# Attention with a memory term, then routed experts, on one core: K and Q turned by TensorE instead of the DMA queue, and one pool of five PSUM banks

## The chip, the cores and the metric

The kernel runs on one core of a Trainium2 chip. The metric is the device time of one execution in microseconds (us). A core has TensorE (PE in the rows; PEld is its weight load), VectorE (DVE), ScalarE (ACT), GpSimd (POOL) and SyncE (SP), which here only issues DMAs, one after the other in the order in which they stand in its program. Sixteen DMA engines move the data.

## The reference

Inputs are q, k and v of shape 8 x 8 x 576 x 64 (batches, heads, rows, depth), a memory M of 64 x 64 and a vector z per batch and head, and the weights of eight experts. In brief:

```python
scores = q @ k.T / 8                       # causal, 576 x 576 per head
local  = softmax(scores) @ v
q_p    = where(q > 0, q, exp(q) - 1) + 1   # phi
mem    = (q_p @ M) / (q_p @ z)
x      = g * mem + (1 - g) * local         # g = sigmoid(beta), per head
# routing: the 4608 rows of x go to 8 experts of capacity 576, best score first
out[rows of e] = maximum(x @ w1[e], 0) @ w2[e]
```

The order of the routing depends on x @ w_gate, so the attention has to be precise: each float32 number is carried as two float16 halves, high and low (`h` and `l` in the names).

## The kernel before, in words

The program has two parts. `attention` works through 16 units; a unit is four heads of one batch. `moe_all` follows it and is not touched by the change.

In a unit K, Q and V are loaded (`kf`, `qf`, `vf`, 32-bit). ACT, DVE or POOL split them: the high half is a cast, the low half a subtraction. The two halves of K stand side by side in a tile `h16` of 18 blocks of 128 columns, and likewise those of Q; both have to be turned (rows to columns) before TensorE can use them. The turned tiles are `kT` and `qT`. In units 1 to 15 one DMA transpose of all 18 blocks does it (line 794); in unit 0 TensorE does it (line 787) and the blocks are copied out of PSUM. Then 64 partitions of `kT` are copied into `kB` (DVE) and 64 partitions of `qT` into `qM` (ACT). phi of Q goes the same way into `pT`, by a DMA transpose.

Then come the maxima: TensorE multiplies `qM` by `kT` into a PSUM bank (`pm`), DVE reduces the bank (line 807), 13 banks in a unit. The maxima are turned and written into row 64 of `qM` by a small DMA (line 866), so that the scores come out with the maximum subtracted. The scores go into PSUM banks `st`, twelve in a unit; ACT takes exp of each twice, once to float16 (`ph`, line 941) and once to float32 (lines 945, 948), and the difference `pl` is made by DVE (line 946) or POOL (line 949). `ph` and `pl` times V, and phi times M, gather in `avs`; DVE divides (lines 988 to 999), the result is split again into `xs`, turned by a DMA transpose into `xT` (line 1008) for the gate logits, and written to DRAM as `xd`.

PSUM has two banks `pm` (maxima, small turnings, logits), three banks `st` (scores, turnings of unit 0) and three for `avs`.

The order of everything in `attention` comes from a planner, `Sched`. Each piece of work is a node with the engines that it may run on and a cost in ns on each; `run` places one node after the other by earliest start and by priority. The priorities are tables of numbers (`PR['off']`, and `PR['dl']` for single units); `PR['bias']` and `PR['pin']` choose between engines. Only the order and the choice of engine reach the chip: each engine then executes its own list in that order and waits by semaphores.

Of the kernel before, what the change touches and what calls it, by code (L numbers as in the profile page):

```python
# [8 lines left out]
F32 = mybir.dt.float32  # L9
# [14 lines left out]
          'kba': -12673.13,  # L24
          'kbd': 29586.98,
          'kbv': -25704.42,
          'kha': -15364.72,
          'khp': -12539.24,
          'khv': -3684.87,
          'klp': -5840.71,  # L30
          'klv': -5300.46,
          'mh2a': -3643.2,
          'mh2v': -10560.2,
          'mha': 4609.58,
          'mhv': 3127.63,
          'mlp': 10679.73,
          'mlv': 10869.94,
          'mra': -14972.51,
          'mrv': -26064.0,
          'mza': 11663.77,  # L40
          'mzv': 5122.68,
          'nap': -923.34,
          'nav': -3267.9,
          'nca': -3175.08,
          'ncp': 457.98,
          'ncv': -3705.71,
          'nsp': -4400.74,
          'nsv': 7885.89,
          'p2p': 3448.83,
          'p2v': -5.41,  # L50
          'p4sp': -16452.05,
          'p4sv': -7016.64,
          'pha': 888.22,
          'php': 8134.1,
          'phra': -13218.83,
          'phrv': 14272.35,
          'phv': -6326.42,
          'plp': 4097.89,
          'plv': 4394.03,
          'prepca': -4983.65,  # L60
          'prepcv': 10793.59,
          'qha': -15522.63,
          'qhp': -3121.95,
          'qhv': 2344.84,
          'qlp': -238.04,
          'qlv': 12285.04,
          'qmovea': 2067.13,
          'qmovev': -1201.49,
          'tea': -3562.47,
          'tev': -3884.84,  # L70
          'vha': 10327.79,
          'vhp': -9961.82,
          'vhv': -5992.86,
          'vlp': -5727.56,
          'vlv': 6154.88,
          'xtea': -11851.0,
          'xtev': -7724.13},
 'dl': {'0': {'AV': 85.12,
              'MX': -176.12,
              'N': -174.88,  # L80
              'P2': -232.53,
              'S': -115.14,
              'fin1': 7.89,
              'fin2': 136.19,
              'kb': -101.7,
              'kh': -240.29,
              'kl': -254.81,
              'kt': -109.58,
              'lk': -219.52,
              'lm': -178.54,  # L90
              'lq': -173.13,
              'lv': -176.91,
              'maxrem': -181.54,
              'mfin': 1.0,
              'mfin2': -278.46,
              'mfin3': -235.61,
              'mh': -252.27,
              'ml': 217.86,
              'mz': -301.17,
              'nadd': -276.57,  # L100
              'ncast': -70.14,
              'nsub': -175.89,
              'ph': -94.62,
              'phe': -545.98,
              'phr': -91.1,
              'phs': -192.45,
              'pl': -160.08,
# [1381 lines left out]
```

## Time and profile before

| | us |
|---|---|
| median of three runs | 992.35 (989.7 to 994.24) |
| the profiled execution, its own time | 989.19 |
| its span, first to last instruction | 987.4 |
| attention, 0 to 517 us of the span | 517 |
| experts, from 517 us on | 470.4 |

Over the span PE is busy 80%, DVE 73%, ACT 59% and POOL 54%; the mean granted TensorE clock is 0.914 of full speed. These shares mix the two parts, so the attention is read on its own below.

### The profile page before, as it was taken

What the parts mean: (1) busy time and instruction counts of PE and PEld (TensorE: products, weight loads), DVE (VectorE), ACT (ScalarE), POOL (GpSimd) and SP (SyncE); (2) the same over time, 40 slices, a digit from 0 to 9 for tenths busy, and PEclk for the clock granted to TensorE, in tenths of its full rate; (3) what the DMA queues carried; (4) which work ended last, traced back from release to release, by engine and by line L of the source; (5) the groups of instructions that cost most, each with busy time, mean ns of one, the idle gap of its engine ahead of it and who ended that gap; (6) DMA issues with size and microseconds to landing.
All of it is one profiled execution on the core that took longest, in us unless ns stands there. A gap on an engine that the chain in (4) does not pass through costs nothing.

```text
span 987.4 us, 23446 instructions
## 1 busy us (share of the span) xinstructions
PE 788.5 (80%) x8908; PEld 494.3 (50%) x8908; DVE 724.1 (73%) x2355; ACT 585.4 (59%) x1010; POOL 537.2 (54%) x492
## 2 busy tenths in 40 slices
PE   3466777867777787677861389999999999999995
PEld 2254555656656566555650254444444444444442
DVE  8888889978889898788878887787787777702010
ACT  4366766658777787656743376574746574655110
POOL 6357766757678775645630134655554555496101
PEclk9986979879899899979995599999999999999998
DMA  5679777989888888875240506363647354693101
GB/s 131 98 150 180 156 153 151 191 160 168 171 154 174 158 167 173 164 146 119 39 105 11 213 7 221 101 220 100 216 106 230 86 204 118 224 269 106 46 12 37
DMA packets 336583, 139.08 MB, mean 141 GB/s; under 512 B 306262, under 2 KB 315478, under 8 KB 336470
## 3 DMA queue, kind: packets, MB, share of 16 engines
q1 hardware_dynamic: 330581, 118.71, 53.2%
q0 software_dynamic: 5888, 18.88, 5.8%
q8 instruction: 69, 1.13, 0.5%
q14 instruction: 45, 0.36, 0.1%
HBM read 72.40 MB, written 18.87 MB: 92 GB/s over the span
## 4 chain that ended last, share of the span: by engine, by line
PE 54%; DVE 21%; DMA 9%; issue 5%; SPq 4%; POOL 3%; ACT 3%; POOLq 0%; DVEq 0%; ACTq 0%
PE py L1138 19%; PE ph L1138 17%; PE avs L647 7%; PE st L647 4%; DVE mx L807 4%; PE pm L647 3%; DVE xt L999 2%; PE prem L1138 2%; SPq L707 2%; DMA xT<-xs 2%; DVE pl L946 2%; DVE scr L1372 2%; DMA qT<-h 2%; DMA pT<-p 1%; DMA kT<-h 1%
## 5 line engine op out<-in xcount | busy, mean ns | idle before, releaser
L1288 POOL TENSOR_TENSOR wl<-wst,wh 128x1024 f16<-128x1024 f32 x60 | 128.3, 2166 | 90.8 <-ACT wh L1287 76.6
L1138 PE MATMUL ph<-xT,wh 128*128 128x512 f16 (+1 forms) x560 | 162.7, 365 | 0.4 <-DVE hl L1331 0.4
L807 DVE TENSOR_REDUCE mx<-pm 128x1 f32<-128x512 f32 (+4 forms) x273 | 134.1, 525 | 14.5 <-PE pm L647 14.2
L941 ACT ACTIVATE ph<-st 128x512 f16<-128x512 f32 x192 | 114.1, 594 | 48.0 <-PE st L647 19.7
L647 PE MATMUL st<-qT,kT 128*128 128x64 f16 (+3 forms) x576 | 112.1, 258 | 26.9 <-DVE pl L946 20.6
L949 POOL TENSOR_TENSOR pl<-pf,ph 128x512 f16<-128x512 f32 x80 | 95.2, 1194 | 61.8 <-ACT pf L948 53.5
L647 PE MATMUL avs<-V,ph 128*128 128x65 f16 x1792 | 114.5, 203 | 17.1 <-DVE de L988 5.2
L647 PE MATMUL pm<-kT,qM 128*128 128x384 f16 (+5 forms) x384 | 91.1, 329 | 39.6 <-DVE mx L807 21.7
L647 PEld LDWEIGHTS <-ph 128*128 128x128 f16 x1792 | 104.2, 105 | 26.3 <-issue 23.0
L647 PE MATMUL avs<-V,pl 128*128 128x65 f16 x896 | 109.6, 206 | 0.0
L647 PE MATMUL st<-qM,kB 128*128 128x64 f16 (+3 forms) x576 | 107.6, 257 | 2.1 <-DMA qM<-mrx 1.8
L1350 POOL DMA_INDIRECT out_dram<-ys,idx x40 | 39.0, 976 | 109.8 <-ACT ys L1345 57.8
L1138 PE MATMUL ph<-xT,wl 128*128 128x512 f16 (+1 forms) x280 | 98.4, 365 | 0.0
L1138 PE MATMUL py<-wh,hh 128*128 128x512 f16 x256 | 97.0, 379 | 0.0
L1138 PE MATMUL py<-wl,hh 128*128 128x512 f16 x256 | 97.0, 379 | 0.0
L1138 PEld LDWEIGHTS <-wh 128*128 128x128 f16 x1072 | 68.2, 98 | 57.1 <-issue 1.9
L1138 PE MATMUL prem<-xT,wh 128*128 128x64 f16 x512 | 96.6, 193 | 0.0
L1330 ACT ACTIVATE hh<-ph 128x512 f16<-128x512 f32 x64 | 38.0, 595 | 92.3 <-PE ph L1138 69.0
L647 PEld LDWEIGHTS <-pl 128*128 128x128 f16 x896 | 91.2, 105 | 0.0
L1331 DVE SCALAR_TENSOR_TENSOR hl<-ph,hh 128x512 f16<-128x512 f32 x64 | 43.8, 686 | 60.5 <-ACT hh L1330 59.7
L1372 DVE TENSOR_SCALAR_CACHE_REDUCE scr<-p_LwT,th 128x320 f16<-128x320 f32 x168 | 85.2, 543 | 2.5
L647 PEld LDWEIGHTS <-identb 128*128 128x128 bf16 (+1 forms) x640 | 61.6, 109 | 45.5 <-issue 33.1
(283 smaller groups left out, 2122.2 us busy)
## 6 DMA issues: line engine op xcount, KB each, us to landing
wst<-in_moe_w_dram SPq DMA_DIRECT2D x32, 1024.0 KB
kf<-in_k_dram SPq DMA_DIRECT2D x64, 128.0 KB
qf<-in_q_dram SPq DMA_DIRECT2D x64, 128.0 KB
vf<-in_v_dram SPq DMA_DIRECT2D x64, 128.0 KB
xd<-xs SPq DMA_DIRECT2D x16, 512.0 KB
kf<-in_k_dram SPq DMA_DIRECT2D x32, 32.0 KB
qf<-in_q_dram SPq DMA_DIRECT2D x32, 32.0 KB
mf<-in_M_prev_dram SPq DMA_DIRECT2D x16, 64.0 KB
```

The costliest lines, as they stand in the source:

```text
L647: def MM(*a,**kw): mm(*a,skip_group_check=True,**kw)
L707: SC.add('l'+nm,dq(728,hw=450),lambda x,h=h,s=s: nc.sync.dma_start(out=t[:,4*h:4*h+4,:],in_=s),w=K(nm+'f',u%2,4*h,4*h+4),prio=pr('l'+nm,u, ...
L807: R=lambda o,i: nc.vector.tensor_reduce(o,i,axis=mybir.AxisListType.X,op=ALU.max)
L941: c=SC.add('Eh',[('A',478)],lambda x,a=a: nc.scalar.activation(phs_[x.buf['ph']][:,0:512],stb[a.buf['st']],AF.Exp,scale=0.125),acq=('ph',) ...
L946: e=SC.add('P2v',[('V',602)],lambda x,a=a,c=c: nc.vector.tensor_sub(pls_[c.buf['ph']][:,0:512],stb[a.buf['st']],phs_[c.buf['ph']][:,0:512] ...
L949: e=SC.add('P2',[('P',1113)],lambda x,c=c,d=d: nc.gpsimd.tensor_sub(pls_[c.buf['ph']][:,0:512],pfs[d.buf['pf']],phs_[c.buf['ph']][:,0:512] ...
L1138: def MM(*a,**kw): mm(*a,skip_group_check=True,**kw)
L1288: SC.add('sp',[('P',2079)],lambda x,ws=ws,k=k,s=s: G_.tensor_sub(wl[:,k,s],ws(),wh[:,k,s]),r=[key+('h',)],w=[key+('l',)],after=[b],rel=rel ...
L1330: b=SC.add('hh',[('A',478)],lambda x,a0=a0,f=f: A_.activation(hh[:,f],phb[a0.buf['ph']],AF.Relu),w=[('hh',f)],after=[y],prio=pr('hh',n,pos ...
L1331: SC.add('hl',[('V',602)],lambda x,a0=a0,f=f: V_.scalar_tensor_tensor(hl[:,f],phb[a0.buf['ph']],0.0,hh[:,f],op0=ALU.max,op1=ALU.subtract), ...
L1350: z=SC.add('scat',[('P',655 if i<4 else 330,'p',0,(1034,'n'))],lambda x,e=e,i=i,r_=r_: G_.indirect_dma_start(out=out,out_offset=bass.Indir ...
L1372: V(462,lambda x,j=j,t_=t_,c_=c_: V_.tensor_scalar(scr[j],LwT,t_[:,j+1:j+2],0.0,op0=ALU.is_ge,op1=ALU.add,accum_out=c_[:,j:j+1]),r=['LwT', ...
```

## The change

The halves of K and Q of every unit are turned by TensorE, in pieces of 8, 8 and 2 blocks, and copied from PSUM into `kT` and `qT` by ACT or DVE. `qT` to `qM` may now be moved by a DMA, and is, in units 1 to 15. phi and the outputs are still turned by the DMA queue. `pm` and `st` become one pool `pb` of five banks. Low halves are made in pieces of 8 and 10 blocks instead of 9 and 9. The planner's costs for DMAs and for two other nodes are changed, and its tables are new: `dl` has entries for all 16 units, and `pin` puts other work on other engines.

```diff
-    def run(self,tol=100,sem=170,same=110,t0=0.0,hwg=450,dlat=1300,dend=950,ph=2800.0,thr=3060):
+    def run(self,tol=100,sem=170,same=110,t0=0.0,hwg=450,dlat=1300,dend=950,ph=2800.0,thr=3060,pel=60):
...
-                    st_=max(dmaf,q); free[e]=st_+1089 if kind=='t' else s2+25
+                    st_=max(dmaf,q); free[e]=st_+1500 if kind=='t' else s2+25
...
-    pmb=[ps.tile([128,512],F32,name=f'pm{i}') for i in range(2)]; stb=[ps.tile([128,512],F32,name=f'st{i}') for i in range(3)]
+    pbb=[ps.tile([128,512],F32,name=f'pb{i}') for i in range(5)]
...
-            SC.add('l'+nm,dq(728,hw=450),lambda x,h=h,s=s: nc.sync.dma_start(out=t[:,4*h:4*h+4,:],in_=s),
+            SC.add('l'+nm,dq(728,hw=530),lambda x,h=h,s=s: nc.sync.dma_start(out=t[:,4*h:4*h+4,:],in_=s),
...
+    def PTT(u): return UO(u).get('ptt') or P_.get('ptt','')
+    def MVP(u): return PCP(u) if u==0 else P_.get('mvp') or [[0,18]]
+    def PCP(u): return UO(u).get('pc_p') or P_.get('pc_p') or [[0,8],[8,16],[16,18]]
...
-            if nm in UO(u).get('ptt',''):
+            if nm in PTT(u):
...
-                        p=stb[x.buf['st']].bitcast(F16)
+                        p=pbb[x.buf['pb']].bitcast(F16)
                         for i in range(a,b_): nc.tensor.transpose(p[:,128*(i-a):128*(i-a)+128],g()[:,i],cst['idh'])
...
-                x_=SC.add(nm+'t',dq(112*(b_-a),kind='t'),lambda x,a=a,b_=b_: nc.sync.dma_start_transpose(
+                x_=SC.add(nm+'t',dq(176*(b_-a),kind='t'),lambda x,a=a,b_=b_: nc.sync.dma_start_transpose(
...
-            SC.add('qmove',al('qmove',u,v=..,a=..), ... cp(x.var,qM[u%3][0:64,a:b_],qTs[U3][64:128,a:b_])
+            SC.add('qmove',al('qmove',u,d=819*(b_-a)/18+60,v=..,a=..), ... nc.sync.dma_start(out=qM[u%3][0:64,a:b_],in_=qTs[U3][64:128,a:b_]) if x.var=='d' else cp(...)
...
-                n3=SC.add('N3',[('V',680)],f,
+                n3=SC.add('N3',[('V',970)],f,
...
- 'pin': {'kh': 'a', 'ph': 'a', 'phr': 'a', 'vh': 'a', 'qmove': 'a', 'ns': 'p**v',
+ 'pin': {'kh': '*', 'ph': 'p', 'phr': 'v', 'vh': 'p', 'qmove': 'dvvv', 'ns': 'ppp*', 'te': '*a*aa*a**aa*',
...
+ 'ptt': 'kq',
```

Every `pmb` and `stb` of the rest becomes `pbb`.

Three places show what moves. The first is SP's list in the middle of the attention (`kf`, `qf`, `vf` are loads, `xd` the outputs; 128x18x128 is a whole unit). Before:

```order
L794 DMA_TRANSPOSE pT_122<-p_115 128x18x128
L707 DMA vf_109<-in_v_dram 128x4x64 x2
L711 DMA vf_109<-in_v_dram 64x2x64 x2
L707 DMA kf_104<-in_k_dram 128x4x64 x4
L712 DMA kf_104<-in_k_dram 64x2x64 x2
L1008 DMA_TRANSPOSE xT_167<-xs_165 128x20x128
L794 DMA_TRANSPOSE qT_121<-h_113 128x18x128
L804 DMA qM_100<-qM_100 1x16x144
L1021 DMA xd<-xs_165 64x512
L1022 DMA xd<-xs_165 128x4x512
L794 DMA_TRANSPOSE kT_118<-h_114 128x18x128
```

The same part of SP's list in the changed kernel:

```order
L1200 DMA_TRANSPOSE pT_123<-p_115 128x18x128
L1169 DMA mf_125<-in_M_prev_dram 64x4x64
L1110 DMA vf_109<-in_v_dram 128x4x64 x4
L1114 DMA vf_109<-in_v_dram 64x2x64 x2
L1414 DMA_TRANSPOSE xT_168<-xs_164 128x20x128
L1210 DMA qM_99<-qM_99 1x16x144
L1427 DMA xd<-xs_164 64x512
L1428 DMA xd<-xs_164 128x4x512
L1208 DMA qM_99<-qT_120 64x2304
L1110 DMA qf_107<-in_q_dram 128x4x64 x4
```

Two of the four transposes of a unit are gone, and a move of 64 partitions (line 1208) stands in the list instead; over the whole list 15 + 15 transposes leave and 15 moves come.

The second place is ACT's list, again in the middle. Before, the exps of the scores with the move of Q and the cast of V between them:

```order
L877 ACTIVATE ef_110<-ef_110 128x1152
L689 COPY qM_98<-qT_119 64x2304
L941 ACTIVATE ph_130<-st_175 128x512
L689 CAST V_101<-vf_108 128x20x64
L945 ACTIVATE st_175<-st_175 128x512
L941 ACTIVATE ph_136<-st_176 128x512
```

After:

```order
L1321 ACTIVATE p4h_151<-pb_176 128x128
L1347 ACTIVATE ph_131<-pb_177 128x512
L1322 ACTIVATE p4f<-pb_176 128x128
L1092 COPY kT_116<-pb_173 128x1024
L1092 COPY kT_116<-pb_174 128x256
L1347 ACTIVATE ph_134<-pb_175 128x512
```

The move of Q and the cast of V have left ACT, and the copies of the turned blocks out of PSUM have come: 60 of 128x1024 and 30 of 128x256 in the program, all on ACT, beside eight smaller ones of unit 0.

The third place is DVE's list (`mx` are the reductions of the maxima, `xt` and `de` the division, `pl` a low half of the scores). Before:

```order
L807 TENSOR_REDUCE mx_155<-pm_174 128x1
L996 TENSOR_TENSOR xt_162<-avs,de_160 128x320
L807 TENSOR_REDUCE mx_155<-pm_173 128x1
L946 TENSOR_TENSOR pl_143<-st_175,ph_135 128x512
L1033 COPY lt_170<-pm_174 128x40
L999 SCALAR_TENSOR_TENSOR xt_162<-avs,de_160,xt_162 128x64 x5
L1037 TENSOR_TENSOR lt_170<-lt_170,pm_174 128x40
L807 TENSOR_REDUCE mx_155<-pm_173 128x1 x2
```

After:

```order
L1405 SCALAR_TENSOR_TENSOR xt_162<-avs,de_160,xt_162 128x64 x5
L1213 TENSOR_REDUCE mx_156<-pb_177 128x1
L1213 TENSOR_REDUCE mx_156<-pb_174 128x1 x2
L1213 TENSOR_REDUCE mx_156<-pb_173 128x1
L1213 TENSOR_REDUCE mx_156<-pb_175 128x1 x2
L1213 TENSOR_REDUCE mx_156<-pb_176 128x2
L1213 TENSOR_REDUCE mx_156<-pb_174 128x1
```

Before, other work stands between nearly all the reductions; after, those of a unit follow one another over all five banks. In TensorE's list the 209 banks of maxima came in 82 runs of one bank, 46 of two and six longer ones before, a run being what stands between two pieces of scores or products; after there are 24 of one, 10 of two and 32 longer ones, of up to 13. The last maxima stand eight heads ahead of the end before, and twelve after.

Summed over the lists, DVE issues 2051 instructions before and 2068 after, ACT 928 and 942, POOL 497 and 541. Per unit 1 to 15 the casts of V and phi go from ACT to POOL, the relu of phi from ACT to DVE; 15 subtractions `xs` go from DVE to POOL, and low halves of K from DVE (6 to 2) to POOL.

## Rows read from the trace of the kernel before

**Rows 1.** Busy time of each engine in two stretches, the attention and the experts: stretch in us, its length, busy us (instructions) by engine, then the granted clock, the share of the DMA engines and GB/s.
```profile
0.00:517.00 517.00, 370.89 (x6077) 287.25 (x6077) 437.47 (x1109) 348.34 (x600) 330.65 (x351) 0.89 0.76 148
517.00:987.40 470.40, 417.57 (x2831) 207.09 (x2831) 286.65 (x1246) 237.11 (x411) 206.53 (x141) 0.94 0.42 133
```

**Rows 2.** The instructions in order of time, ACT: the small cast that ends the maxima of a unit, of unit 1 and of unit 15 (start, duration).
```profile
67.31 0.25 ACT L689 CAST mr<-pm 18x128 f16<-18x128 f32 x1
...
482.14 0.25 ACT L689 CAST mr<-pm 18x128 f16<-18x128 f32 x1 [1.02 <-PE pm L859]
```

**Rows 3.** Busy time between those two casts and behind the second (columns PE, PEld, DVE, ACT, POOL, clock, DMA share, GB/s), and in the stretch where DVE is busiest.
```profile
67.31:482.14 414.83, 311.18 (x5157) 243.15 (x5157) 353.58 (x898) 294.55 (x506) 279.32 (x272) 0.87 0.81 158
482.14:517.40 35.26, 24.27 (x556) 20.64 (x553) 26.70 (x88) 20.33 (x41) 15.90 (x17) 0.99 0.40 75
...
350.00:375.00 25.00, 20.66 (x400) 16.54 (x399) 23.82 (x63) 19.89 (x36) 17.96 (x17) 1.00 0.89 171
```

**Rows 4.** SP's list in order of time: start, duration of the issue, what is issued.
```profile
262.74 3.42 SPq L794 DMA_TRANSPOSE qT<-h  x1
266.25 0.61 SPq L804 DMA_DIRECT2D qM<-qM  x1
266.92 0.58 SPq L1021 DMA_DIRECT2D xd<-xs  x1
267.55 0.58 SPq L1022 DMA_DIRECT2D xd<-xs  x1
268.18 3.72 SPq L794 DMA_TRANSPOSE kT<-h  x1
271.95 1.17 SPq L707 DMA_DIRECT2D kf<-in_k_dram  x2
273.16 2.23 SPq L712 DMA_DIRECT2D kf<-in_k_dram  x2
```

**Rows 5.** The same issues by line, over the whole program: min/median/max in ns, first and last start.
```profile
L794 SPq DMA_TRANSPOSE kT<-h x15: 2704/2856/4440, 25.4 to 431.2; - x15
L794 SPq DMA_TRANSPOSE qT<-h x15: 2621/3005/3582, 38.8 to 445.7; - x15
L794 SPq DMA_TRANSPOSE pT<-p x17: 1231/3104/4651, 21.2 to 476.8; - x17
L1008 SPq DMA_TRANSPOSE xT<-xs x15: 3038/3120/3652, 87.6 to 498.9; - x15
L707 SPq DMA_DIRECT2D kf<-in_k_dram x64: 448/513/1577, 0.7 to 398.0; - x64
L712 SPq DMA_DIRECT2D kf<-in_k_dram x32: 599/607/1521, 1.8 to 399.3; - x32
```

**Rows 6.** The chain that ended last, by line, as shares of the span.
```profile
PE py L1138 19%; PE ph L1138 17%; PE avs L647 7%; PE st L647 4%; DVE mx L807 4%; PE pm L647 3%; DVE xt L999 2%; PE prem L1138 2%; SPq L707 2%; DMA xT<-xs 2%; DVE pl L946 2%; DVE scr L1372 2%; DMA qT<-h 2%; DMA pT<-p 1%; DMA kT<-h 1%
```

**Rows 7.** DMA around one transpose of 18 blocks, which is issued at 476.84 us and has nothing beside it: stretches as in rows 1.
```profile
478.00:480.00 2.00, 1.02 (x19) 0.75 (x18) 1.87 (x6) 2.00 (x5) 1.99 (x3) 1.00 1.17 196
480.00:482.00 2.00, 1.73 (x36) 1.35 (x35) 1.94 (x8) 0.67 (x2) 1.46 (x2) 1.00 0.57 99
```

**Rows 8.** ACT's groups, shapes apart: count, busy us and mean ns, idle time before them.
```profile
L689 ACT COPY qM<-qT 64x2304 f16<-64x2304 f16 x15 | 31.7, 2110 | 17.3 <-DMA qT<-h 17.1
L689 ACT CAST V<-vf 128x1280 f16<-128x1280 f32 x15 | 19.4, 1293 | 2.6 <-PE avs L647 2.5
L876 ACT ACTIVATE ef<-qf 128x1152 f32<-128x1152 f32 x15 | 17.5, 1165 | 2.7 <-POOL p L778 2.5
L689 ACT CAST p<-ef 128x1152 f16<-128x1152 f32 x15 | 17.3, 1152 | 31.1 <-DVE ef L878 18.9 <-DMA pT<-p 12.3
L689 ACT COPY xT<-pm 128x640 f16<-128x640 f16 x3 | 2.1, 692 | 2.9 <-PE pm L1017 2.9
L1258 ACT COPY xT<-py 128x512 f16<-128x512 f16 x5 | 2.8, 586 | 7.3 <-DVE xT L1257 7.3
```

**Rows 9.** Groups of DVE and POOL, likewise.
```profile
L1002 DVE TENSOR_TENSOR xs<-xt,xs 128x320 f16<-128x320 f32 x15 | 10.3, 690 | 0.1
L690 DVE CAST h<-qf 128x1152 f16<-128x1152 f32 x15 | 13.2, 878 | 5.9 <-DMA qT<-h 3.8 <-issue 1.5 <-DMA xd<-xs 0.6
L778 DVE TENSOR_TENSOR h<-kf,h 128x576 f16<-128x576 f32 x6 | 8.9, 1488 | 0.0
L691 POOL TENSOR_SCALAR V<-vf 128x768 f16<-128x768 f32 x1 | 0.8, 842 | 0.0
L691 POOL TENSOR_SCALAR V<-vf 128x512 f16<-128x512 f32 x1 | 0.6, 624 | 0.0
L1002 POOL TENSOR_TENSOR xs<-xt,xs 128x320 f16<-128x320 f32 x49 | 45.3, 927 | 38.2 <-DVE xs L690 26.0 <-ACT xs L689 8.7 <-PE avs L647 2.7
```

**Rows 10.** Turnings on TensorE that are there already: 36 blocks of unit 0 and 20 of the last outputs (groups), and five of the latter in order of time (start, length of the run of five).
```profile
L787 PE MATMUL st<-idh,h 128*128 128x128 f16 x36 | 4.7, 308 | 9.7 <-POOL h L778 8.7 <-DVE qT L690 0.9
L1017 PE MATMUL pm<-idh,xs 128*128 128x128 f16 x20 | 1.8, 218 | 2.4 <-DVE xs L690 2.3
...
507.61 0.44 PE L1017 MATMUL pm<-idh,xs 128*128 128x128 f16 x5
```

**Rows 11.** The first step of the division on DVE, in order of time: the first and the last of the eight heads behind the last maxima.
```profile
483.26 0.17 DVE L988 SCALAR_TENSOR_TENSOR de<-avs,eps 128x10 f32<-128x10 f32 x1 [0.50 <-PE avs L647]
...
512.69 0.17 DVE L988 SCALAR_TENSOR_TENSOR de<-avs,eps 128x10 f32<-128x10 f32 x1 [1.67 <-PE avs L647]
```

More of the change, by code (lines that the diff above doesn't have):

```diff
@@ L41 @@
-          'mzv': 5122.68,
+          'kba': -26568.09,
+          'kbd': 40635.67,
+          'kbv': -61697.16,
+          'kha': -51687.37,
+          'khp': 22485.47,
+          'khv': -5643.82,
+          'klp': -44101.74,
+          'klv': -46879.6,
+          'mh2a': 23202.08,
+          'mh2v': 41742.42,
+          'mha': -803.96,
+          'mhv': -17250.11,
+          'mlp': 32467.03,
+          'mlv': 3444.98,
+          'mra': 23705.05,
+          'mrv': -33461.43,
+          'mza': -15047.4,
@@ new lines @@
+          'p4sp': -13422.2,
+          'p4sv': 18348.44,
+          'pha': -2666.63,
+          'php': 109708.75,
+          'phra': 29855.7,
+          'phrv': 24082.96,
+          'phv': 1286.06,
+          'plp': 4127.93,
+          'plv': 4521.49,
+          'prepca': -28993.02,
+          'prepcv': -42440.6,
+          'qha': -15602.67,
+          'qhp': 56435.17,
+          'qhv': 61680.59,
+          'qlp': -22555.44,
+          'qlv': 26102.73,
+          'qmovea': 25183.32,
+          'qmoved': -25040.81,
@@ L362 @@
- 'p2k': 'vpvpvvpvpvpv',
- 'pin': {'kb': '*',
-         'kh': 'a',
-         'kl': '**',
+ 'off': {'AV': 371.78,
+         'MX': -79.91,
+         'N': -79.8,
+         'P2': 100.74,
+         'S': 133.16,
+         'fin1': 141.18,
+         'fin2': -418.14,
+         'kb': -419.68,
+         'kh': 625.0,
+         'kl': -953.14,
+         'kt': -24.07,
+         'lk': 46.04,
+         'lm': 337.59,
+         'lq': 16.21,
+         'lv': 73.06,
+         'maxrem': -7.9,
+         'mfin': -321.35,
+         'mfin2': -556.91,
+         'mfin3': 39.45,
+         'mh': 153.33,
+         'ml': -2137.2,
+         'mz': 433.6,
+         'nadd': -788.91,
+         'ncast': 333.82,
+         'nsub': 342.69,
+         'ph': -1500.4,
+         'phe': 282.51,
+         'phr': -150.77,
+         'phs': -181.76,
+         'pl': 857.91,
+         'prep': -119.19,
+         'proc24': 898.96,
+         'pt': 21.25,
+         'qh': -980.0,
+         'ql': -390.16,
+         'qmove': -3.11,
+         'qt': -421.12,
+         'sj4': -190.05,
+         'vh': 895.22,
+         'vl': -55.77},
@@ L380 @@
-         'pl': '**',
-         'prepc': 'a',
+         'phr': 'v',
+         'pl': '**p',
+         'prepc': 'v',
          'qh': 'v',
-         'ql': 'pp',
-         'qmove': 'a',
-         'vh': 'a',
-         'vl': '**',
-         'xte': 'a*v*'},
- 'run': {'tol': 0},
+         'ql': '*pv',
+         'qmove': 'dvvv',
+         'te': '*a*aa*a**aa*',
+         'vh': 'p',
+         'vl': 'ppv',
+         'xte': 'a**v'},
+ 'ptt': 'kq',
+ 'run': {'tol': 0.9},
  'strict': 1,
@@ L604, in run @@
                 js=len(j.alts)==1 and j.alts[0][0]==e and dma is None
-                g=f+((0 if e=='T' else same) if js else sem)
+                g=f+((0 if e=='T' else same) if js else sem+pel*(e=='T'))
                 if dma is not None: g=f+50
```

1102 lines of the change are left out of this document (716 added, 386 removed).

## The prediction, made before the changed kernel ran

> **What bounds the kernel now.** I read the stretches first: the experts take 470 of the 987 us and are not touched, so only the 517 us of attention can move [rows 1]. Next the pace: the small cast that ends the maxima of a unit comes at 67.31 us for unit 1 and at 482.14 us for unit 15, so 14 units take 414.83 us, 29.63 us each [rows 2]. In that steady part DVE is busy 353.58 us (85%), PE 311.18 (75%), ACT 294.55 (71%), POOL 279.32 (67%), and the DMA engines 81% [rows 3]. No engine that computes is full; DVE is nearest. In its best stretch of 25 us it was busy 23.82, or 95% [rows 3], so 85% is not its ceiling.
>
> Then the queue that has no busy column, SP's. In rows 4 seven groups of issues follow one another from 262.74 to 275.39 us and fill 12.31 of these 12.65 us. Summed over a unit by medians [rows 5]: the four transposes 2.86 + 3.00 + 3.10 + 3.12 = 12.1 us, twelve loads at 0.51 = 6.2, six half-height loads at 0.61 = 3.7, and five small ones at about 0.6 [rows 4] = 3.0. That is 25.0 of 29.63 us, 84% by medians; in a stretch like rows 4 it is 97%. A transpose is issued for as long as five or six loads, and everything behind it waits in order.
>
> The chain agrees that this queue matters: it holds DMA qT with 2%, DMA kT with 1% and SP's issue of loads with 2% [rows 6]. Rounded as they are, that is 5% of 987, 49 us, all in the attention. DVE and PE hold most of the rest of the attention's chain.
>
> **Removed.** 30 transposes. SP loses 2.86 + 3.00 = 5.9 us of issue in each of 15 units and gets one move of 64 partitions, which I price like the half-height load, 0.6. SP falls to 25.0 - 5.3 = 19.7 us, 66% of a unit. The DMA engines: one transpose of 18 blocks costs 2 x 1.17 + 2 x 0.57 = 3.5 us of all sixteen [rows 7], two are 7.0 us of the 24.0 (81% of 29.63) that a unit uses now. The move carries half the bytes of a transpose: between nothing and those 3.5 us, I take half, 1.7. The DMA share falls to about 63%. So all 49 us of that chain can go; how much is kept depends on what lies right behind, which is DVE.
>
> **Added on PE.** 15 units x 36 = 540 turnings. Five of them in a row take 0.44 us with the last lasting 0.218, so one follows the other after 0.055 us [rows 10]; the 36 of unit 0 make 4.7 us, 0.13 each with their ends [rows 10]. That is 30 to 70 us. The steady part has a granted clock of 0.87, nearer to the fast row, so I take 0.083 each, 45 us. PE's lines hold 7 + 4 + 3 = 14% of 987 us, 138 us, of the attention's chain [rows 6], which is 27% of 517: of the 45 us about 12 lie on the path (8 to 19).
>
> **Added and taken away on ACT.** Out go the move of Q, the cast of V, the relu and the cast of phi: 31.7 + 19.4 + 17.5 + 17.3 = 86 us [rows 8]. In come 60 copies of 1024 and 30 of 256 columns out of PSUM. From 692 ns for 640 and 586 for 512 [rows 8] a column costs 0.83 ns, so 1024 cost 1.01 us and 256 0.37: 61 + 11 = 72 us, and about 5 in unit 0. ACT is about 9 us lighter. On the path: nothing, with its 29% of idle time as cover. If that cover were gone, a bank would be held 1.0 us longer for each copy and the maxima and scores would wait for it.
>
> **POOL.** From 842 and 624 ns for 768 and 512 columns [rows 9] the casts of V (1280) and phi (1152) cost 1.28 and 1.17 us: 37 us in 15 units. 15 subtractions of `xs` at 927 ns add 14 [rows 9]; the new cut of the low halves takes some 5 off. POOL is 46 us heavier: (279 + 43)/415 = 78%, still below DVE, so nothing on the path. Its cover is its 33% of idle time; gone, `pl` from POOL comes late and the products of a head wait.
>
> **DVE.** Off: 15 `xs` at 690 ns (10.3) and four low halves of K at 1.49 (6.0) [rows 9], and eight copies of unit 0, about 3.5. On: 15 relus. No row shows one on DVE; the cast of the same 1152 columns, 878 ns [rows 9], is the nearest, 13.2 us, and between 0 and twice that is the bound. Seven more casts of `xs` and four more low halves of phi add about 10 at prices like these. Together +4 us (-9 to +17), of which I put 1 on the path.
>
> **The move of Q.** It was 2.11 us on ACT [rows 8], now a DMA: 0.6 of issue at least, and at most that with the 3.5 us of a whole transpose [rows 7] behind it. The difference is -1.5 to +2 a unit. It is a wait of `qM`, thus of the maxima, which stand a unit ahead of the scores; I take 0. It does put a new wait into SP's list: the move waits for ACT's copies of `qT`, and the loads and the transposes of phi and the outputs stand behind it. With a third of the queue free that costs nothing as long as the loads run a unit ahead.
>
> **The sum.** The steady part: DVE's 353.58 us plus its share of the 4 us are 357. Losing all 49 us would make DVE 357/366 = 98% busy, above its best. At 95% the part takes 375 us, so at most 40 us can be kept; at least none. I take 34, which leaves DVE at 94%, since rows 3 show that DVE holds such a share for 25 us at a time. Then +12 (PE) +1 (DVE): -21. At the end, four more heads run without maxima beside them. A head takes (512.69 - 483.26)/7 = 4.20 us there [rows 11], and DVE is 26.70/35.26 = 76% busy [rows 3] and not 85: 16.8 us x 0.09 = +1.5. Total -20 us (-19.5). The profiled execution takes 989.19 us, 1.8 us more than its span, and becomes 969; the median of the runs shown is 3 us above it, and from it the same step gives **972 us**, which I predict.
>
> **Rivals.**
> *Hidden anyway.* Right behind the queue's chain lies one through DVE and PE, only 15 us shorter; the added 13 to 15 us eat it: 990 to 994. For it: with 85% busy, DVE leaves just 61 us of idle time in the steady part [rows 3]. Against: the stretch at 95% shows the same work packed closer.
>
> *Slower, by the clock.* Maxima come in long runs now, with DVE's reduction setting the pace, and TensorE sits between them; turnings are short bursts that wait for POOL's halves. If TensorE is busy less evenly and the granted clock of the steady part falls from 0.87 to 0.80, its 311 us become 338, and the turnings at the slow price (70 x 14/15 = 65) make it 403: at a share of 94% the part takes 429 us, +14, and the time is about 1007. It decides from the point where PE passes 94% of 415, 390 us: a clock of 0.83. Against it: in the stretch at the end, where five turnings took 0.44 us, the clock was 0.99 [rows 3, 10].
>
> *Slower, turnings that do not overlap.* If each turning took its whole 0.308 us [rows 10], 540 would cost 166 us, PE would need 311 + 155 = 466 us for the steady part, 51 more than it takes now, and the time would be 1043 with PE never idle. Rows 10 speak against it. This is near to what the Trainium skill says ("TensorE: Matmul & The Clock Gate", Part 4: PE-mode transpose): about 275 ns for one in a kernel, and the full clock does not engage for this mode; by its figure 149 us would be added, an estimate from that page. The trace disagrees on the sum: 20 turnings made 1.8 us busy, 0.09 each.
>
> *More gain.* DVE keeps 95% and the turnings fall into PE's idle 25%: -40 and another -5 for two transposes in the start, 947.
>
> **How the numbers follow.** A change of 0.5% (5 us) is about what a measurement of this kernel can tell. Chances: the forecast 0.50 (its own range 958 to 985), more gain 0.11, hidden anyway 0.17, the clock 0.19, turnings that do not overlap 0.03. So faster 0.61, same 0.17, slower 0.22. The range for 8 in 10 leaves out the lowest part of "more gain" and the upper half of the clock's case: 946 to 1006.
>
> **What would show it.** Right: SP's list with gaps in a stretch like rows 4; the casts of rows 2 about 28.2 us apart; DVE above 88% in the steady part; no DMA kT or qT in the chain; groups of five or eight turnings with 0.06 to 0.09 us between starts. Wrong: the pace still at 29.6 with SP idle (hidden anyway); a clock at or below 0.83 with PE above 90% (the clock); ACT's copies as what the maxima or scores wait for, or `pl` of POOL as what the products wait for: then a cover that I counted on is gone.

## The result: slower, not faster

The changed kernel takes 1002.76 us (1001.72 to 1004.61) and the kernel before, on the same chip, 991.03 (987.13 to 994.24): a ratio of 1.0122, interval 1.0081 to 1.0164. I had predicted 972 and gave "slower" 0.22. The time lies inside the range, but the sign was wrong and none of my rivals describes what happened.

The profiled execution of the changed kernel took 1001.72 us. The stretches that answer to [rows 1] (columns: length, then busy us and instructions of PE, PEld, DVE, ACT, POOL, then clock, DMA share, GB/s):

```profile
0.00:523.70 523.70, 389.16 (x6617) 308.67 (x6617) 456.71 (x1125) 328.90 (x615) 383.71 (x395) 0.91 0.57 121
523.70:999.90 476.20, 418.77 (x2831) 207.91 (x2831) 289.05 (x1248) 236.69 (x409) 205.52 (x141) 0.93 0.41 132
```

The attention is 6.7 us longer and the experts 5.8. The two casts of [rows 2] stand at 72.70 and 470.29 us, and the stretches between and behind them, as in [rows 3]:

```profile
72.70:470.29 397.59, 308.31 (x5283) 243.08 (x5281) 356.77 (x869) 256.86 (x483) 309.25 (x297) 0.93 0.59 126
470.29:523.70 53.41, 38.54 (x804) 33.18 (x802) 37.46 (x115) 29.36 (x61) 28.59 (x31) 0.89 0.31 71
```

The maxima now come every 28.40 us (I had said 28.2) and DVE is 90% busy, as I wanted. But the part behind them grew from 35 to 53 us: the maxima ran further ahead while the heads stayed behind. The last head, which began at 512.69 in [rows 11], begins here:

```profile
518.19 0.17 DVE L1394 SCALAR_TENSOR_TENSOR de<-avs,eps 128x10 f32<-128x10 f32 x1 [2.05 <-PE avs L1050]
```

The queue was relieved. In the stretch that answers to [rows 4], SP now has gaps of 3.1, 1.0 and 3.9 us:

```profile
261.64 1.44 SPq L1115 DMA_DIRECT2D qf<-in_q_dram  x2
266.20 2.28 SPq L1110 DMA_DIRECT2D kf<-in_k_dram  x4
268.53 1.27 SPq L1115 DMA_DIRECT2D kf<-in_k_dram  x2
270.76 0.60 SPq L1169 DMA_DIRECT2D mf<-in_M_prev_dram  x1
275.24 3.14 SPq L1414 DMA_TRANSPOSE xT<-xs  x1
```

And the chain that ended last, by engine. First the kernel before, then the changed one:

```profile
PE 54%; DVE 21%; DMA 9%; issue 5%; SPq 4%; POOL 3%; ACT 3%; POOLq 0%; DVEq 0%; ACTq 0%
```

```profile
PE 53%; DVE 31%; issue 4%; ACT 3%; DMA 3%; POOL 3%; SPq 2%; DVEq 0%; POOLq 0%; ACTq 0%
```

DMA and SP's queue lost 8 points together, 79 us, and DVE took 10, about 100 us. So the chain did not get shorter; it moved to DVE. By line, in the changed kernel:

```profile
PE py L1544 18%; PE ph L1544 16%; DVE mx L1213 7%; PE avs L1050 7%; PE pb L1050 6%; DVE xt L1405 3%; DVE pl L1352 3%; PE prem L1544 2%; DVE mh L1093 2%; DVE scr L1778 2%; DVE xt L1402 1%; DVE ef L1282 1%; SPq L1110 1%; DMA qf<-in_q_dram 1%; PE pb L1193 1%
```

The largest growth is in the reductions `mx`, 7% where [rows 6] has 4, which are the same work as before. `mh` and `ef` were not in [rows 6]. What became of these two is in the groups (window 60 to 460 us, mean ns behind the busy us). Before, where the relu is not on DVE:

```profile
L690 DVE COPY mh<-mh 64x260 f16<-64x260 f16 x12 | 6.2, 516 | 0.3
```

Changed:

```profile
L1093 DVE COPY mh<-mh 64x260 f16<-64x260 f16 x14 | 19.2, 1372 | 0.4
L1282 DVE TENSOR_SCALAR ef<-qf 128x1152 f32<-128x1152 f32 x13 | 17.0, 1309 | 0.3 <-DVE de L1394 0.3
L1093 DVE COPY mf<-zT 64x4 f32<-64x4 f32 x13 | 5.6, 433 | 0.1
```

`mf` holds the memory M and z of a unit, `mh` its high half; the copy puts that half on partitions 64 to 127 as well. It is the same instruction in both kernels, and it became 2.7 times as long. The copy of a column into `mf` is new on DVE: before, ACT made 15 of the 16 at 0.19 us each, and the section on the change does not list this move. The reason for the long copies shows in one of them. DVE and POOL in order of time (start, duration):

```profile
302.41 5.94 DVE L1093 COPY mh<-mh 64x260 f16<-64x260 f16 x1
...
301.72 1.18 POOL L1290 TENSOR_TENSOR ml<-mf,mh 64x260 f16<-64x260 f32 x1
302.87 2.26 POOL L1355 TENSOR_TENSOR pl<-pf,ph 128x512 f16<-128x512 f32 x2
305.10 1.53 POOL L1408 TENSOR_TENSOR xs<-xt,xs 128x320 f16<-128x320 f32 x2
306.59 0.42 POOL L1323 TENSOR_TENSOR p4l<-p4f,p4h 128x128 f16<-128x128 f32 x1
306.98 1.28 POOL L1094 TENSOR_SCALAR V<-vf 128x1280 f16<-128x1280 f32 x1
308.35 2.59 POOL L1299 TENSOR_TENSOR V<-vf,V 128x512 f16<-128x512 f32 x2
```

POOL works without a gap through seven instructions. The last of them, a cast of V that the change put there, ends at 306.98 + 1.28 = 308.26, and the copy ends at 308.35, 0.09 us later. It is the same with a relu:

```profile
372.46 4.46 DVE L1282 TENSOR_SCALAR ef<-qf 128x1152 f32<-128x1152 f32 x1
...
372.09 1.28 POOL L1094 TENSOR_SCALAR V<-vf 128x1280 f16<-128x1280 f32 x1
373.34 0.42 POOL L1323 TENSOR_TENSOR p4l<-p4f,p4h 128x128 f16<-128x128 f32 x1
373.73 2.58 POOL L1299 TENSOR_TENSOR V<-vf,V 128x512 f16<-128x512 f32 x2
377.48 1.15 POOL L1094 TENSOR_SCALAR p<-ef 128x1152 f16<-128x1152 f32 x1 [1.17 <-DMA pT<-p]
```

POOL pauses at 376.31 and the relu ends at 376.92, 0.61 us later. Of the copies of `mh` and the relus over 1 us between 60 and 490 us, twelve in all, the seven copies end 0.07 to 0.09 us behind the end of an instruction of POOL, and the five relus 0.60 to 0.62 behind one. That is a DVE instruction that counts as busy while it waits for POOL, and then does the rest of its own work.

DVE does not always have to wait for a pause of POOL. In nine of the twelve POOL paused there, for 0.07 us or more; in the other three its next instruction had begun about 0.03 us before. One of these:

```profile
244.37 3.17 DVE L1093 COPY mh<-mh 64x260 f16<-64x260 f16 x1
...
244.19 0.67 POOL L1290 TENSOR_TENSOR ml<-mf,mh 64x260 f16<-64x260 f32 x1
244.82 1.39 POOL L1184 TENSOR_TENSOR p<-ef,p 128x640 f16<-128x640 f32 x1
246.19 1.28 POOL L1094 TENSOR_SCALAR V<-vf 128x1280 f16<-128x1280 f32 x1
247.43 0.42 POOL L1323 TENSOR_TENSOR p4l<-p4f,p4h 128x128 f16<-128x128 f32 x1
```

This copy passed two such boundaries and ended just behind the third, at 247.54, when `p4l` was already running; the one of 5.94 us passed six. At which of them DVE gets in, no run tells.

The Trainium skill has this rule ("SBUF — State Buffer", section "Who interferes with whom"): DVE and GpSimd share one pair of SBUF ports, copies, casts and `tensor_scalar` on DVE can need it, and whoever comes first has it for its whole instruction. The trace agrees on the wait. On its length the measurement goes further: the wait can be longer than one instruction, and the 5.94 us here cover seven of POOL.

### The profile page after: what moved, and what is told of

It reads as the page before. It is cut to its first block, busy times and chain, and to the rows that moved or that the text cites. A ratio compares the mean times of both kernels' runs of the same rounds, so it can differ in the third digit from the quotient of the medians.

```text
span 999.9 us, 24617 instructions
## 1 busy us (share of the span) xinstructions
PE 807.9 (81%) x9448; PEld 516.6 (52%) x9448; DVE 745.8 (75%) x2372; ACT 565.6 (57%) x1024; POOL 589.2 (59%) x536
## 4 chain that ended last, share of the span: by engine, by line
PE 53%; DVE 31%; issue 4%; ACT 3%; DMA 3%; POOL 3%; SPq 2%; DVEq 0%; POOLq 0%; ACTq 0%
PE py L1544 18%; PE ph L1544 16%; DVE mx L1213 7%; PE avs L1050 7%; PE pb L1050 6%; DVE xt L1405 3%; DVE pl L1352 3%; PE prem L1544 2%; DVE mh L1093 2%; DVE scr L1778 2%; DVE xt L1402 1%; DVE ef L1282 1%; SPq L1110 1%; DMA qf<-in_q_dram 1%; PE pb L1193 1%
## 5 line engine op out<-in xcount | busy, mean ns | idle before, releaser
L1347 ACT ACTIVATE ph<-pb 128x512 f16<-128x512 f32 x192 | 114.9, 601 | 76.3 <-PE pb L1050 61.1
L1213 DVE TENSOR_REDUCE mx<-pb 128x1 f32<-128x512 f32 (+5 forms) x273 | 128.2, 527 | 4.1 <-PE pb L1050 3.2
L1050 PE MATMUL avs<-V,ph 128*128 128x65 f16 x1792 | 107.8, 197 | 26.8 <-DVE xt L1405 15.3
L1050 PE MATMUL pb<-qT,kT 128*128 128x64 f16 (+3 forms) x576 | 106.6, 252 | 22.1 <-DVE pl L1352 16.5
L1355 POOL TENSOR_TENSOR pl<-pf,ph 128x512 f16<-128x512 f32 x80 | 100.0, 1259 | 40.0 <-ACT pf L1354 39.8
L1050 PEld LDWEIGHTS <-ph 128*128 128x128 f16 x1792 | 98.8, 101 | 37.8 <-issue 34.0
L1050 PE MATMUL pb<-kT,qM 128*128 128x256 f16 (+5 forms) x384 | 82.2, 316 | 28.2 <-DVE mx L1213 14.9
L1050 PE MATMUL pb<-qM,kB 128*128 128x64 f16 (+3 forms) x576 | 103.4, 251 | 1.3 <-DMA qM<-mrx 1.3
L1050 PE MATMUL avs<-V,pl 128*128 128x65 f16 x896 | 103.3, 200 | 0.0
L1776 ACT ACTIVATE scs<-p_LwT,th 128x320 f16<-128x320 f32 x84 | 47.0, 560 | 66.6 <-DVE th L1785 51.0
```

Source lines behind the costliest of these rows:

```text
L1050: def MM(*a,**kw): mm(*a,skip_group_check=True,**kw)
L1213: R=lambda o,i: nc.vector.tensor_reduce(o,i,axis=mybir.AxisListType.X,op=ALU.max)
L1347: c=SC.add('Eh',[('A',478)],lambda x,a=a: nc.scalar.activation(phs_[x.buf['ph']][:,0:512],pbb[a.buf['pb']],AF.Exp,scale=0.125),acq=('ph',) ...
L1355: e=SC.add('P2',[('P',1113)],lambda x,c=c,d=d: nc.gpsimd.tensor_sub(pls_[c.buf['ph']][:,0:512],pfs[d.buf['pf']],phs_[c.buf['ph']][:,0:512] ...
L1776: SC.add('sign',[('A',547)],lambda x,j=j,t_=t_,c_=c_: A_.activation(scs[j-KV],LwT,AF.Sign,bias=t_[:,4:5],accum_out=c_[:,j:j+1]),r=['LwT',( ...
```

## The experiments

The theory: DVE waits inside some of its instructions from SBUF to SBUF, since POOL's runs became longer and DVE got the relu as well. Rivals: the experts' new order; TensorE's turnings; DVE simply full; a relief of the queue that was worth little. In all that moves work between engines, the order of each list is kept as planned, and only the engine that executes is another. Differences between two runs are taken between their ratios to the kernel before, times 992 us; with the intervals given they are good to about 5 us.

**The experts.** My text ahead of the prediction says that the change does not touch them. That was wrong: both parts are planned by the same `run`, whose defaults changed, and its lists on DVE, ACT and POOL are in another order. Here the experts get the old costs (`tx` stands for the 1500 of a transpose).

```diff
-    for x in SC.run(ph=P_.get('ph',5000.0),**P_.get('run',{})): x.fn(x)
+    for x in SC.run(ph=P_.get('ph',5000.0),pel=0,tx=1089,**P_.get('run',{})): x.fn(x)
```

> The changed kernel, with the attention's order as it is; only the planner of the experts' part gets the two old costs back (a transpose holds the queue for 1089 instead of 1500 ns, no extra 60 ns behind TensorE), which gives the experts' part the order that it had before. Theory: 5 to 6 of the 11.7 us come from this re-ordering, since the experts' part took 470.4 us before and 476.2 after: about 997 us, and 470 us behind the last output of the attention. Rival: the experts' part is longer because of how the attention leaves the chip (clock, queues): 1003, no change.

1005.18 us, ratio 1.013 (1.0085 to 1.0175): no gain. The counterpart, the kernel before with the new costs for the experts alone:

> The kernel before with the experts' part planned with the two new costs, so that its lists are those of the changed kernel; the attention is that of before. After the last head the single executions showed 474.7 us before, 481.7 changed, and 478.5 and 476.5 with the experts' old order. If the order costs 3 us or more: 0.3 to 0.7% slower than before. If not: within 0.2% of before.

Ratio 1.0013 (0.9989 to 1.0037). The new order costs between -1 and +4 us, so not the 12. Behind the last head the single profiles show 474.7 to 479.5 us with the old order (six kernels) and 478.0 to 481.8 with the new one (eleven); of the 7 us between the two profiles shown, about 3 may be the order, and the rest lies within the spread of single profiles.

**DVE's three instructions to ACT.** The relu of phi, the upper copy of `mh` and the copy of a column into `mf`:

```diff
-   (nc.scalar.activation(ef[U2][:,a:b_],qf[U2][:,a:b_],AF.Relu,scale=-1.0) if x.var=='a' else
+   (nc.scalar.activation(ef[U2][:,a:b_],qf[U2][:,a:b_],AF.Relu,scale=-1.0) if x.var in 'av' else
...
-   cp(x.var,mf[U2][:,:,64],zT[0:64,4*u:4*u+4])
+   cp('a',mf[U2][:,:,64],zT[0:64,4*u:4*u+4])
...
-   cp(x.var,mhs[U2][64:128],mhs[U2][0:64])
+   cp('a',mhs[U2][64:128],mhs[U2][0:64])
```

> The changed kernel with every instruction at its place in the order, but three small works of a unit done by ACT instead of DVE: the relu of phi (mean 1247 ns on DVE, up to 4465), the copy of mh to the upper partitions (mean 1467, up to 5937) and the copy of z into mf (440). Theory: DVE waits inside these instructions while POOL works, DVE is the engine that sets the pace at 90% busy, and this ate what the queue gave: attention 15 to 25 us shorter, 978 to 988 us. Rival (TensorE's turnings, or the order of the maxima, set the pace): within 4 us of 1003, since ACT gets 26 us more and DVE's idle time grows.

981.39 us, ratio 0.9891 (0.9856 to 0.9927): 23 us better than the changed kernel and faster than both. With the relu alone, or the two copies alone:

> The changed kernel with the relu of phi alone (15 x 128x1152) on ACT instead of DVE. The changed kernel takes 1002.8, and with relu, mh copy and mf copy all on ACT 981.4. Theory (DVE waits inside instructions from SBUF to SBUF until GpSimd's list has a gap; what counts is the time that stands in the chain, 2.7% for the relu against 4.2% for the mh copy in the stretch 30 to 523 us, 13 and 21 us, of which the run before returned 62%): 994 to 995. Rival (DVE is simply full, what counts is the work, and only the relu is work that is new to DVE): nearly all of the 21 us, 982 to 985.

> The changed kernel with the copy of the upper half of mh (64x260) and the copy of the column of mf (64x4) alone on ACT, the relu stays on DVE. The first of the two was on DVE in the kernel before as well, at 544 ns in the mean against 1467. Theory (waiting for gaps of GpSimd): 988 to 991, the larger half of the 21 us. Rival (DVE full by its new work): a gain like that of 7 us of work without waits, 996 to 1002.

0.9989 (0.9965 to 1.0012) and 0.9974 (0.9949 to 0.9999): 13 and 15 us below the changed kernel. The relu gave more than the 8 us that the theory expected and less than the 18 to 21 of its rival, the copies what the theory expected. 13 + 15 is more than 23; why the halves overlap was not tested. Neither half does it all, so "only the relu is new work" falls: the copy of `mh` was there before, and taking it away with the small one of `mf` is worth as much as the relu.

**POOL's casts back to ACT.**

```diff
-   cp(x.var,g()[:,a:b_,hcol],srcs[U2][:,a:b_])
+   cp('a' if nm=='p' else x.var,g()[:,a:b_,hcol],srcs[U2][:,a:b_])
-   cp(x.var,V16[U2][:,a:b_,65:129],vf[U2][:,a:b_])
+   cp('a' if u else x.var,V16[U2][:,a:b_,65:129],vf[U2][:,a:b_])
```

> The changed kernel with every instruction at its place in the order, but the casts of V and of phi in units 1 to 15 done by ACT as before, not by POOL (POOL 38 us lighter, ACT 37 us heavier). Theory: POOL's load is what makes DVE's copies wait: the copy of mh falls from 1467 ns towards the 262 ns median of before, the relu towards 760, and the time by 8 to 18 us, 985 to 995. Rival: POOL has no part in it, the DVE rows keep their durations and the time stays within 4 us of 1003 or grows by ACT's load.

994.29 us, ratio 1.0012 (0.9986 to 1.0038): 11 us better than the changed kernel, though DVE's list is the same to the instruction and ACT has 37 us more to do. A DVE that is full by its list alone does not explain that. DVE's two groups shrank with POOL's work:

```profile
L1093 DVE COPY mh<-mh 64x260 f16<-64x260 f16 x14 | 13.5, 962 | 1.0 <-ACT mh L1092 0.6
L1282 DVE TENSOR_SCALAR ef<-qf 128x1152 f32<-128x1152 f32 x13 | 11.4, 877 | 0.0
```

**The same moves in the kernel before.** Nothing else of the change, K and Q turned by DMA: relu on DVE (that of unit 0 too), casts of V and phi on POOL (`x.var` replaced at the same places).

> The kernel before with nothing of the change but three moves between engines, in units 1 to 15: the relu of phi on DVE, the casts of V and of phi on GpSimd. Theory (DVE waits in its instructions from SBUF to SBUF while GpSimd works without a gap, whoever turns K and Q): the copy of mh, 544 ns in the mean before, goes above 900, the relu above 1000, and the time is 6 to 14 us above the kernel before. Rival (the waits come from the new order of the changed kernel): both durations stay near 544 and 880, and the time is within 5 us of before, or below it, since ACT loses 54 us of work.

1012.59 us, ratio 1.0172 (1.0138 to 1.0206), 17 us slower and more than the 6 to 14 expected, although ACT lost 54 us of work. The groups:

```profile
L876 DVE TENSOR_SCALAR ef<-qf 128x1152 f32<-128x1152 f32 x13 | 18.9, 1457 | 1.0 <-DMA qf<-in_q_dram 0.9
L690 DVE COPY kB<-kT 64x2304 f16<-64x2304 f16 x12 | 16.8, 1402 | 0.0
L690 DVE COPY mh<-mh 64x260 f16<-64x260 f16 x12 | 13.8, 1149 | 0.3
```

The waits come with the engine moves, whoever turns K and Q. Without the relu on DVE:

> The kernel before with the casts of V and phi alone on GpSimd in units 1 to 15 (37 us off ACT), the relu stays on ACT. With the relu on DVE as well it was 1.017 of before. If the longer runs of GpSimd do the damage by themselves: 1.006 or more, with the mean of the mh copy near 1100 ns. If it takes new work of DVE from SBUF to SBUF beside them: 0.995 to 1.004.

```profile
L690 DVE COPY mh<-mh 64x260 f16<-64x260 f16 x12 | 13.4, 1114 | 0.3
```

Ratio 1.0032 (1.0005 to 1.0059): the copy is as long as with the relu, but that costs just 3 us, with ACT relieved of 37 us of casts. It takes DVE's additional work to make 17 of it. The relu on DVE costs 14 us here, beside the casts on POOL, and 13 in the changed kernel.

**What the queue's relief was worth.** In the kernel before, plain DMA copies of the same bytes in place of the 30 transposes:

```diff
-   nc.sync.dma_start_transpose(out=T_[ti][:,a:b_],in_=fl(g()[:,a:b_]))
+   (nc.sync.dma_start(out=T_[ti][:,a:b_],in_=g()[:,a:b_]) if nm in 'kq' else nc.sync.dma_start_transpose(...))
```

> The kernel before with the 30 DMA transposes of K and Q in units 1 to 15 replaced by plain DMA copies of the same bytes, so K and Q stay unturned there and the scores are other numbers; all the work of the engines stays. This takes the issue and most of the transfer time of the transposes away and adds nothing. Prediction's term (34 us kept of the queue's 49 in the chain, at most 40): 950 to 960. Theory (other chains lie right behind): a gain of 0 to 15 us, 975 to 990.

974.23 us, ratio 0.9804 (0.9783 to 0.9826): 19 us, between the two expectations. The copies still stand in SP's list, at 0.5 to 0.6 us of issue each in the median, so this is a little less than the whole relief. The chain's DMA share fell and DVE's rose:

```profile
PE 56%; DVE 28%; DMA 5%; issue 4%; ACT 3%; SPq 3%; POOL 1%; another core or an unknown queue 0%; DVEq 0%; POOLq 0%; ACTq 0%
```

In busy time (60 to 460 us) DVE stands at 90% there:

```profile
60.00:460.00 400.00, 308.50 (x5216) 240.20 (x5215) 360.34 (x908) 300.01 (x513) 283.31 (x274) 0.88 0.71 165
```

From the other side I loaded the queue again, in the kernel with the three instructions on ACT:

```diff
+   if u and [a,b_]==list(ch_[-1]):
+       for c in range(6): nc.sync.dma_start(out=cst['scr'][2*u+(nm=='q')][:,3*c:3*c+3],in_=g()[:,3*c:3*c+3])
```

> The changed kernel with relu, mh copy and mf copy on ACT (0.989 of before), with the queue loaded again: after the turnings of K and of Q of units 1 to 15 six plain DMAs of 98 KB each write the halves to a spare place in DRAM, about 6 us of issue in a unit, as much as the two transposes took. If the relief of the queue is worth 34 us: 1010 or more. If it is worth little because other chains lie right behind: 0 to 12 us slower than without, 982 to 994.

1070.87 us, ratio 1.0769 (1.0735 to 1.0803), far beyond both. It is no price of the relief alone: these DMAs hold the tile of halves, and the next unit's casts wait for them, a wait which the kernel without them does not have. Waits, 60 to 460 us (total us, times, longest):

```profile
DVE h L1093 <- DMA scr<-h: 38.0, 7, 7.6
...
ACT h L1092 <- DMA scr<-h: 23.9, 5, 9.2
```

Its worth here stays unmeasured in that direction.

**What ate the 19 us.** The changed kernel with all these engines undone, so that it mostly differs from the kernel before in who turns K and Q:

> The changed kernel with relu, mh copy and mf copy on ACT and the casts of V and phi on ACT as well: K and Q are turned by TensorE, but this work is shared out about as in the kernel before. The casts alone gave 8.5 us, the three DVE works alone 21.4. Theory (both gains come from the same waits of DVE for GpSimd, so they do not add up): 976 to 981. Rival 1 (two separate causes, DVE's work and GpSimd's work): 973 or below. Rival 2 (ACT, 358 us busy in the first 530 us with the three works, becomes the bound with 33 us more): 985 or more.

988.26 us, ratio 1.0005 (0.9977 to 1.0032): with these engines undone the change brings nothing, and with the casts on POOL the same kernel is 11 us better (0.9891). The time is that of rival 2, ACT as the bound; of ACT as the bound the trace shows 78% busy (60 to 460 us) and 10% of the chain, against 3% in the changed kernel. Its chain by engine:

```profile
PE 54%; DVE 20%; ACT 10%; issue 5%; DMA 4%; POOL 2%; SPq 1%; DVEq 0%; POOLq 0%; ACTq 0%
```

If the queue's relief is worth its 19 us here too, something that came with the turning costs as much. That it is the turning itself is argued and not shown: the new order, the common pool of banks, the move of Q by DMA, 15 `xs` and low halves of K on POOL, and here the copy of `mh` on ACT differ as well. The turning has two parts, TensorE's work and ACT's copies out of PSUM. I doubled each. First TensorE's, in the changed kernel:

```diff
-   for i in range(a,b_): nc.tensor.transpose(...)
+   for i in [i for i in range(a,b_) for _ in range(2 if u else 1)]: nc.tensor.transpose(...)
```

> The changed kernel with each of the 540 turnings of K and Q in units 1 to 15 issued twice into the same place (the second overwrites the first with the same values): 46 us more work on TensorE, nothing else. Theory (DVE sets the pace): 3 to 12 us longer, 1006 to 1015. Rival (TensorE sets the pace, and the turnings ate the gain): 30 us or more, 1033 and above.

1004.82 us, ratio 1.0118 (1.0071 to 1.0164): nothing, less than both expectations. I took DVE to stand in front there, so I went to the kernel with the three instructions on ACT:

> The changed kernel with relu, mh copy and mf copy on ACT (0.989 of before), with each of the 540 turnings of units 1 to 15 issued twice, about 46 us more for TensorE. In the changed kernel itself the same doubling cost 2 us, but there DVE stood in front. If TensorE's turnings are what ate the 19 us that the plain copies gave: 1.005 to 1.01 of before (10 to 20 us more). If not: at most 0.993.

Ratio 0.9989 (0.9961 to 1.0017), 10 us more, a ratio between the two expected. TensorE's turnings count once DVE is out of the way, but for no more than half of the 19, if the first 540 cost no more than the second. Then the copies, in the same kernel:

```diff
-   cp(x.var,T_[ti][:,a:b_],pbb[p_.buf['pb']]...)
+   [cp(x.var,T_[ti][:,a:b_],pbb[p_.buf['pb']]...) for _ in range(2 if u else 1)]
```

> The same kernel with each copy of turned blocks from PSUM (60 of 1024 columns, 30 of 256, units 1 to 15, on ACT) made twice, 72 us more for ACT. If these copies are what ate the 19 us: 10 us or more above the kernel without the doubling, 1.0 of before or more. If ACT's idle time covers them, as the prediction had it: at most 0.993.

1031.4 us, ratio 1.0385 (1.0349 to 1.0421): 49 us more for 72 us of copies. ACT is 79% busy in the stretch 60 to 460 us and no engine is full, yet ACT's share of the chain is 17%:

```profile
60.00:460.00 400.00, 297.49 (x4791) 231.79 (x4790) 309.73 (x762) 316.90 (x555) 280.35 (x274) 0.90 0.56 118
```

```profile
PE 53%; DVE 19%; ACT 17%; issue 5%; POOL 3%; DMA 2%; SPq 1%; POOLq 0%; DVEq 0%; ACTq 0%
```

TensorE's waits for these copies show why the second costs more than the first. The largest of them (60 to 460 us; total us, times, longest), without the doubling and with it:

```profile
PE pb L1050 <- ACT kT L1092: 2.8, 5, 0.7
...
PE pb L1050 <- ACT kT L1092: 19.7, 21, 1.9
```

All of TensorE's waits for `kT` and `qT` from ACT come to 8 us without the doubling and to 43 with it; in the kernel with all engines undone they are 10, in the changed kernel 4. So 0.68 us per us is the price of more copies, and no price of those that the change made.

**A version of both.** The three instructions on ACT, with the experts' old order:

> The changed kernel with relu, mh copy and mf copy on ACT, and the experts' part planned with the costs of before, so that its lists are those of before. After the last head the kernel before takes 474.7 us, the changed one 481.7, the one with the old order of the experts 478.5, the one with the three works on ACT 480.2. If the order of the experts' lists costs 3 us or more: 975 to 978. If it costs nothing that can be measured: 980 to 983.

981.1 us, ratio 0.9912 (0.988 to 0.9943), the same as 0.9891 with the new order within the intervals. The kernel with the three instructions on ACT is faster than both kernels of this study; the experts' order makes no difference that shows.

## Why the prediction was wrong

Four measured kernels that all turn K and Q by TensorE form a square. Ratios to the kernel before:

| | casts of V and phi on ACT | casts on POOL |
|---|---|---|
| relu, `mh`, `mf` on ACT | 1.0005 | 0.9891 |
| relu, `mh`, `mf` on DVE | 1.0012 | 1.0122, the changed kernel |

Times 992 us, each difference good to about 5 us: alone the three instructions on DVE cost about 1 us, and alone the casts on POOL gain 11. Together they should give -11 and gave +12; 22 us belong to the pair. Part of these is DVE's stretched instructions: between the lower two kernels the busy time of `mh`, `ef` and `mf` on DVE differs by 5.7 + 5.6 + 0.8 = 12 us (60 to 460 us). Another part may be that ACT is relieved by both moves and can use the relief only once; no run separates that. In the first entry of the table the queue's relief, about -19 in the kernel before, is eaten by what came with the turning; this +19 is only a difference, and it compares a kernel in the new order with one in the old. The copy of `mh` was on DVE in the kernel before as well, so the 23 us of the right column are not all cost of work that the change put there.

**The DVE term, "+4 us (-9 to +17), of which I put 1 on the path": the step that turned the sign, together with POOL's.** I priced the two apart. With the casts on ACT, about 1 us is what the relu and the two copies cost on DVE; beside the casts on POOL it is 23, and for the relu alone 13. I priced the relu by the cast of `h`, 878 ns [rows 9]; it took 1309 in the stretch shown, and 877 when POOL had its casts taken away. I did not price the copies at all: that of `mh` stayed where it was and became 2.7 times as long, and the move of `mf` to DVE I left out. Over the attention DVE became 19 us busier, above my upper bound.

**The POOL term, "still below DVE, so nothing on the path".** The price was put in the wrong place. I asked when POOL itself would be late. Its idle time was also DVE's chance to get at SBUF, and I counted that time as free cover. Taking the casts away again gave 11 us. A price row for this stood in the trace of before, where a copy that takes 221 ns at its shortest took 542 in the mean of the 16 and up to 1820; I did not read the spread of one form on DVE.

**The kept gain, "I take 34".** The relief alone gave 19 us, with DVE at 90%. I reasoned from DVE's best 25 us [rows 3] to what it could hold for 400; it did not hold that. This error alone would have left a gain: -20 + 15 is still -5.

**The ACT term, "nothing, with its 29% of idle time as cover".** In the changed kernel that was nearly so: TensorE waited 4 us for the copies between 60 and 460 us. What it costs when ACT has more to do I had named as the price of a lost cover, and gave it no number; the doubling shows 0.68 us of time per us of further copies.

**The PE term, "about 12 lie on the path".** The size was near, but only in another kernel. The turnings together, 0.088 us each where I took 0.083:

```profile
L1193 PE MATMUL pb<-idh,h 128*128 128x128 f16 x576 | 50.9, 242 | 21.6 <-DVE h L1184 11.8 <-DVE mx L1213 3.7 <-DVE pl L1352 3.6
```

Doubled they cost 10 us where DVE was out of the way and nothing in the changed kernel. A run of eight shows that they overlap, which ends the rival of turnings that take their whole time:

```profile
298.43 0.61 PE L1193 MATMUL pb<-idh,h 128*128 128x128 f16 x8
```

**The clock.** The rival with a falling clock is out: it is 0.93 in the steady part, against 0.87 in [rows 3].

**The signs I named.** Gaps in SP's list, casts 28.4 us apart (28.2 forecast), DVE above 88%, turnings 0.056 us apart in the median, no `kT` or `qT` by DMA in the chain: all five came, and the kernel was slower. (The move of `qT` to `qM` by DMA, which I took at 0, does stand in the chain, with 3.5 and 3.1 us.) They tested that the work moved as I thought, not that the time followed. The casts' distance was a bad witness above all, since the maxima can run ahead of the heads. The heads' own pace says at once that nothing was gained: from the ninth head to the 57th it took 349.1 us before and 348.2 after. The first step of their division, two lines of the kernel before, then two of the changed one:

```profile
134.19 0.16 DVE L988 SCALAR_TENSOR_TENSOR de<-avs,eps 128x10 f32<-128x10 f32 x1
483.26 0.17 DVE L988 SCALAR_TENSOR_TENSOR de<-avs,eps 128x10 f32<-128x10 f32 x1 [0.50 <-PE avs L647]
...
136.19 0.16 DVE L1394 SCALAR_TENSOR_TENSOR de<-avs,eps 128x10 f32<-128x10 f32 x1
484.40 0.17 DVE L1394 SCALAR_TENSOR_TENSOR de<-avs,eps 128x10 f32<-128x10 f32 x1 [0.50 <-PE avs L1050]
```

The 12.5 us between the two profiles shown lie outside this stretch: 2.0 ahead of it, 4.4 in the last seven heads and 7.0 behind the last.

## What to carry to other kernels

A busy share of DVE may contain waits. Where one form on DVE from SBUF to SBUF has a wide spread of durations, lay POOL's list beside it. Work moved to POOL and work moved to DVE should be priced as a pair: here the second cost 1 us alone, the first gained 11, and both together cost 12. Such DVE work was better put on ACT here. Idle time of an engine is a cover that runs out: with ACT at 79%, further copies out of PSUM cost 0.68 us for each us.

## What I had not expected of the hardware

A DVE copy of 0.22 us took 5.94 us, through seven instructions of POOL that followed each other without a gap: DVE was let in at none of the six boundaries between them, though in three other cases it got in at one. Reductions from PSUM on DVE did not stretch (`mx` from 512 columns has a mean of 673 ns before and 677 after in the same window), which agrees with the Trainium skill ("SBUF — State Buffer", section "Who interferes with whom": reductions on DVE never contend); nor did the casts of `xs` (477 and 479), which also go from SBUF to SBUF; why those are spared no run here tells.
